# Pooled attention and a two-layer feed-forward on one core: attention in cycles of 4 and 5 key chunks, a new table of issue times, preparation in four banks, weights converted in the last pair, second phase in passes of 2, 4, 4, 4, 2

## The chip, the cores and the metric

One core of one Trainium2 chip runs the whole program. The metric is device time in microseconds (us), the median of several executions. The engines are named as the profile names them: PE (matrix engine, PEld its weight loads), DVE (vector), ACT (scalar), POOL (GpSimd), SP (which issues DMAs).

## The reference

```python
# q, k, v: (4, 8, 1152, 64) float32; w_in (512, 2048), w_out (2048, 512)
q_pool = q.reshape(B, H, S // 2, 2, D).mean(axis=3)        # 576 query rows a head
scores = 1/np.sqrt(D) * np.matmul(q_pool, k.transpose(0, 1, 3, 2))
scores = scores - np.max(scores, axis=-1, keepdims=True)
attn = np.exp(scores)
attn = attn / (np.sum(attn, axis=-1, keepdims=True) + 1e-09)
attn_out = np.matmul(attn, v)                               # (4, 8, 576, 64)
x = attn_out.transpose(0, 2, 1, 3).reshape(2304, 512)
h = np.maximum(x @ w_in, 0.0)
out = (h * h) @ w_out                                       # (2304, 512)
```

## The kernel before, in words

**First phase.** Two heads make a pair, and there are 16 pairs, two heads side by side on the partitions. A pair is worked in two halves `e` of 288 query rows, each over 9 key chunks of 128 keys.
- Preparation: `load_q`, `load_k`, `load_v` issue the DMAs on SP, `pool_q` (L217, L219) adds neighbouring query rows on POOL. `prep` transposes keys and queries on PE into one PSUM bank `t`, `prep_high` (ACT, L256) writes the rounded high part and `prep_low` (DVE, L261, L263) the rest. Five such units a pair share the one bank with the row-maximum transposes and the row sums.
- Row maxima: `maxes` (PE, L285) multiplies queries by keys into one PSUM buffer `m` of two banks, `max_left` (DVE, L297, L293) reduces it; 12 such units a pair. `max_fin` (DVE, L301) ends them, `max_turn` (PE, L308) transposes the result and `max_rows` (ACT, L315) writes it as the rows `mm`.
- Scores: `scores` (PE, L326) makes a chunk's scores minus the maximum in one of two buffers `s`, eight matmuls; `expo` (ACT, L331) writes exp into `p`.
- `pv` (PE, L337) multiplies `p` by v and `pv_x` (ACT, L350) takes the result to `xt`. `add` (POOL, L361) sums the `p` of a half over its chunks, `total` (PE, L366), `total_x` (ACT, L371) and `recip` (DVE, L375) make the reciprocal row sums, `scale_x` (POOL, L380) applies them.
- While a pair's scores run, the next pair is prepared and its maxima are taken.

**The order** of all this is written out by hand: `at(key, ...)` gives each step a time in units of a cycle (here 3 chunks, 6 cycles a pair), with fractions from the table `AT`; a step named in `after` moves a key up. The steps are issued sorted by key, and every engine works its own steps in that order.

**Weights.** The weights arrive as 64-bit numbers; a unit is 128 columns of `w_in` or 128 rows of `w_out`, 32 units in all. `load_raw` loads one, `convert` makes float32 of it in six DVE operations (L119 to L133) and one POOL addition (L135), `split_w` divides it into a high part (ACT, L145) and a low part (DVE, L146).  Eight units are converted in the first phase, from cycle 14 on, one operation a cycle.

**Second phase.** Tokens stand in 5 tiles, one of 256 and four of 512; `f` runs over 16 blocks of 128 hidden columns. `split_x` (ACT L152, DVE L153) divides a token tile into high and low parts. `layer1(i, f)` is 12 matmuls (L507), then a square of the positive part (ACT L509, DVE L511), split again (ACT L514, DVE L515); `layer2` (L543) follows two steps later and adds into four PSUM banks over the blocks of a pass. A pass is 4 blocks (`FP`) over all 5 token tiles, then the sums are copied (ACT L549) or added (DVE L551) to `part`. The units of the next pass are converted during a pass.

Of the kernel before, what the change touches and what calls it, by code (L numbers as in the profile page):

```python
# [21 lines left out]
    s=(.04, .16, .28), e=(.16, .31, .46),  # L22
    xa=0., ra=.06, xb=.40, rb=.47, rf=.50,
    ma=.46, ha=.62, la=.75, mb=.90, hb=1.0, lb=1.34,
    pv=(.55, .66, .77), px=.95,
    a0=.65, a1=.65, a2=.70, a3=.75,
    sm=.92, sc=1.02, sr=(1.8, 2.8), sx=2.9,
    c0=14, cp=1.0, cf=.80,
)
WARM = 16  # L30
# [4 lines left out]
def kernel(  # L35
# [22 lines left out]
    G = 3  # L58
    W = G * P
# [9 lines left out]
    def run(ctx, exact):  # L69
# [6 lines left out]
        xt = [xpool.tile([P, KD, TW[i]], F32, name=f"xt{i}") for i in range(NB)]  # L76

        def x_cols(c0, n):
            while n:
                i, o = divmod(c0 - TW[0] + TB, TB)  # L80
                o -= 0 if i else TB - TW[0]
                m = min(n, TW[i] - o)
                yield i, o, m
                c0 += m
                n -= m
# [7 lines left out]
        FP = 4  # L93
        FX = 2
# [64 lines left out]
        with ExitStack() as a:  # L159

            kq = a.enter_context(tc.tile_pool(name="kq", bufs=1))
            ptp = a.enter_context(tc.tile_pool(name="ptp", bufs=5))
# [15 lines left out]
            PM = [kq.tile([P, 2, NT5, G], F32, name=f"pm{i}") for i in range(2)]  # L178
# [56 lines left out]

            def prep(n, u):
                t = bank(n)
                if u < G:
                    kt = ld_["k", n]
                    for i in range(G):  # L240
                        nc.tensor.transpose(out=t[:, i * P:(i + 1) * P], in_=kt[:, u * G + i].rearrange("p h d -> p (h d)"), identity=ident)
                    b_[n, u] = t[:, :W], [x[:, u * W:(u + 1) * W] for x in KK[n % 2]], 1.0
                else:
                    qp, qpl = qp_[n]
                    rs = range(NR - 1) if u == G else range(NR - 1, NR)
                    for i, r in enumerate(rs):
                        nc.tensor.transpose(out=t[:, i * P:(i + 1) * P], in_=qp[:, r].rearrange("p h d -> p (h d)"), identity=ident)  # L247
                    w = len(rs) * P
                    if u > G:
                        nc.tensor.transpose(out=t[:, w:w + NL], in_=qpl.rearrange("p h d -> p (h d)"), identity=ident[0:NL, 0:NL])  # L250
                        w += NL
                    b_[n, u] = t[:, :w], [x[:, rs[0] * P:rs[0] * P + w] for x in QQ[n % 2]], QS

            def prep_high(n, u):
                x, (hi, lo), sc = b_[n, u]
                nc.scalar.activation(out=hi, in_=x, func=ACTF.Copy, scale=sc)  # L256

            def prep_low(n, u):
                x, (hi, lo), sc = b_.pop((n, u))
                if u < G:  # L260
                    nc.vector.tensor_tensor(out=lo, in0=x, in1=hi, op=ALU.subtract)  # L261
                else:
                    nc.vector.scalar_tensor_tensor(out=lo, in0=x, scalar=sc, in1=hi, op0=ALU.mult, op1=ALU.subtract)  # L263


            units = [(t, g) for t in range(3) for g in range(2)] + [((0, 1, 2), 2)] + \
                    [(t, g) for t in range(3, NT5) for g in range(2)] + [((3, 4), 2)]
# [4 lines left out]
            def maxes(n, u):  # L272
                ts, g = units[u]
                if n == 0 and u < 8 and u % 3:
# [31 lines left out]
            def max_turn(n, e):  # L306
                t = bank(n or e)
                nc.tensor.transpose(out=t[:, :P], in_=NM[n % 2].rearrange("p h t -> p (h t)"), identity=ident)  # L308
# [18 lines left out]

            def expo(n, e, c):
                if c % G == 0:
                    p_[n, e, c // G] = ptp.tile([P, G, 2, NH], F32, tag="p", name="p")  # L330
                nc.scalar.activation(out=p_[n, e, c // G][:, c % G], in_=s_.pop((n, e, c))[:, :, :NH], func=ACTF.Exp)  # L331

            def pv(n, e, c):
                if c == 0:
                    pv_[n, e] = vps.tile([P, 512], F32, tag="pv", name="pv")
                for h in range(2):
                    nc.tensor.matmul(out=pv_[n, e][rows(h), :NH], lhsT=ld_["v", n][:, h, c, :],  # L337
                                     rhs=p_[n, e, c // G][:, c % G, h, :], start=(c == 0), stop=(c == NC - 1))
# [280 lines left out]
```

## Time and profile before

| | |
|---|---|
| median of 3 runs | 1027.32 us (1018.22 to 1029.48) |
| profiled execution, its own time | 1035.19 us |
| its span, first to last instruction | 1033.1 us |
| PE busy / weight loads busy | 913.3 us / 661.8 us |
| DVE, ACT, POOL busy | 669.8, 445.5, 437.4 us |
| mean granted clock of PE | 0.934 |

The busy times are sums over two phases with different limits, so they are read by stretch: the rows of the section below come from the table of stretches, the timeline, and the groups of instructions. A matmul's row ends where its last column is modelled to leave; what the engine needs for one is read from the start of one row to the start of the next. In brackets stands how long an engine sat idle before a row, and what ended that.

### The profile page before, as it was taken

The numbers are of one execution on the slowest core, as the hardware profiler recorded it, in microseconds if no ns is written. First come the engines' busy times: TensorE is split into PE (matmuls) and PEld (weight loads), VectorE is DVE, ScalarE is ACT, GpSimd is POOL, SyncE is SP. The second block draws the span as 40 slices with busy tenths as digits, with TensorE's granted clock in tenths as the row PEclk, the third lists the DMA queues.
The fourth block names the chain that finished last, engine by engine and source line by source line (L and its number), as shares of the span: only waits on it lengthen the run. The fifth ranks groups of instructions, "written<-read, shape, count | busy, mean of one in ns | idle before, by whom it ended". The sixth has DMA issues, their size and how long they took to land.

```text
span 1033.1 us, 15093 instructions
## 1 busy us (share of the span) xinstructions
PE 913.3 (88%) x6162; PEld 661.8 (64%) x6162; DVE 669.8 (65%) x839; ACT 445.5 (43%) x872; POOL 437.4 (42%) x246
## 2 busy tenths in 40 slices
PE   6828888889888888888988987999999999999996
PEld 4515555555455555555655656888888888888885
DVE  5135687877878878756555648764877597754433
ACT  2515545545545444445554554444433333233321
POOL 0623676776766857767676781110111010100000
PEclk6958999989899899899998997999999999999999
DMA  4122113302302311211221000111111011000112
GB/s 114 24 69 67 47 44 90 81 27 74 90 23 67 89 47 24 70 46 26 68 70 44 2 1 21 62 61 42 41 62 41 22 55 48 22 1 21 42 41 85
DMA packets 61967, 50.87 MB, mean 49 GB/s; under 512 B 39104, under 2 KB 49344, under 8 KB 61888
## 3 DMA queue, kind: packets, MB, share of 16 engines
q1 hardware_dynamic: 61088, 48.50, 16.5%
q10 hardware_dynamic: 800, 1.31, 0.4%
q8 instruction: 50, 0.82, 0.3%
q14 instruction: 29, 0.24, 0.1%
HBM read 45.09 MB, written 4.72 MB: 48 GB/s over the span
## 4 chain that ended last, share of the span: by engine, by line
PE 68%; POOL 10%; ACT 9%; DVE 9%; issue 2%; DMA 1%; SPq 0%; ACTq 0%; POOLq 0%
PE o L543 18%; PE h L507 18%; PE pv L337 13%; PE s L326 9%; POOL ts L361 8%; ACT p L331 6%; PE m L285 4%; DVE pm L297 3%; DVE r L133 3%; POOL qp L217 2%; ACT j L228 2%; PE t L366 2%; PE t L247 1%; DVE a L119 1%; ACT kk L256 1%
## 5 line engine op out<-in xcount | busy, mean ns | idle before, releaser
L297 DVE TENSOR_REDUCE pm<-m 128x2 f32<-128x1024 f32 x155 | 189.3, 1221 | 119.1 <-PE m L285 118.5
L331 ACT ACTIVATE p<-s 128x576 f32<-128x576 f32 x288 | 177.3, 650 | 102.6 <-PE s L326 102.6
L326 PE MATMUL s<-qq,kk 64*128 64x288 f32 x1728 | 174.0, 309 | 25.7 <-ACT p L331 25.7
L337 PE MATMUL pv<-p,vt 128*64 128x288 f32 x1152 | 185.5, 464 | 0.0
L361 POOL TENSOR_TENSOR ts<-p 128x1728 f32<-128x1728 f32 x32 | 123.9, 3873 | 139.5 <-ACT p L331 139.5
L543 PE MATMUL o<-wo,gh 128*128 128x512 f32 x576 | 177.8, 390 | 1.2 <-ACT gh L514 1.2
L507 PE MATMUL h<-xhi,wi 128*128 128x512 f32 (+1 forms) x600 | 172.0, 370 | 5.0 <-ACT wi L145 5.0
L326 PEld LDWEIGHTS s<-qq,kk 64*128 64x128 f32 x1728 | 137.8, 189 | 54.2 <-ACT p L331 47.6
L135 POOL TENSOR_TENSOR r<-r,h 128x512 f32<-128x512 f32 x32 | 42.3, 1321 | 251.1 <-DVE r L133 183.1
L361 POOL TENSOR_TENSOR ts<-ts,p 128x1728 f32<-128x1728 f32 x32 | 123.8, 3869 | 27.9 <-ACT p L331 27.9
L507 PEld LDWEIGHTS h<-xhi,wi 128*128 128x128 f32 x600 | 110.8, 190 | 25.5 <-ACT wi L145 5.9
L285 PE MATMUL m<-kk,qq 64*128 64x512 f32 (+1 forms) x470 | 93.9, 425 | 34.6 <-DVE pm L297 26.3
L337 PEld LDWEIGHTS pv<-p,vt 128*64 128x64 f32 x1152 | 82.2, 150 | 65.5 <-issue 30.2
L543 PEld LDWEIGHTS o<-wo,gh 128*128 128x128 f32 x576 | 107.1, 188 | 23.3 <-ACT gh L514 1.9
L543 PE MATMUL o<-wo,gl 128*128 128x512 f32 x288 | 112.1, 389 | 0.0
L507 PE MATMUL h<-xlo,wi 128*128 128x512 f32 (+1 forms) x300 | 110.7, 369 | 0.0
L361 POOL TENSOR_TENSOR ts<-ts 128x576 f32<-128x576 f32 x64 | 94.1, 1470 | 4.0
L514 ACT CAST gh<-g 128x512 fp32r<-128x512 f32 (+1 forms) x80 | 46.3, 579 | 110.1 <-PE o L543 65.9
L285 PEld LDWEIGHTS m<-kk,qq 64*128 64x128 f32 x470 | 44.4, 198 | 71.5 <-DVE pm L297 36.1
L515 DVE TENSOR_TENSOR gl<-g,gh 128x512 fp32r<-128x512 f32 (+1 forms) x80 | 54.3, 678 | 52.1 <-ACT gh L514 51.7
L326 PE MATMUL s<-mm,oner 64*128 64x288 f32 x576 | 87.3, 294 | 0.0
L375 DVE RECIPROCAL r<-r 128x144 f32<-128x144 f32 x64 | 64.5, 1030 | 21.2 <-ACT r L371 21.2
(93 smaller groups left out, 1028.9 us busy)
## 6 DMA issues: line engine op xcount, KB each, us to landing
kt<-in_k_dram SPq DMA_DIRECT2D x32, 288.0 KB, 4.3
vt<-in_v_dram SPq DMA_DIRECT2D x16, 576.0 KB, 3.9
qt<-in_q_dram SPq DMA_DIRECT2D x16, 512.0 KB, 3.9
raw<-in_moe_w_in_dram SPq DMA_DIRECT2D x16, 512.0 KB, 3.8
raw<-in_moe_w_out_dram SPq DMA_DIRECT2D x16, 512.0 KB, 3.5
out_dram<-part SPq DMA_DIRECT2D x8, 256.0 KB, 2.6
out_dram<-part ACTq DMA_DIRECT2D x10, 128.0 KB, 3.3
out_dram<-part SPq DMA_DIRECT2D x10, 128.0 KB, 2.7
```

Of the source, the lines that this page charges most:

```text
L135: nc.gpsimd.tensor_tensor(out=r, in0=r, in1=h.bitcast(F32), op=ALU.add)
L285: nc.tensor.matmul(out=m[:, h, o], lhsT=l[rows(h), TQ[t]:TQ[t] + P], rhs=r[rows(h), ks], start=(x == 0), stop=(x == len(terms) - 1))
L297: nc.vector.tensor_reduce(out=pm[:, :, ts, g], in_=m, op=ALU.max, axis=AX.X, negate=True)
L326: nc.tensor.matmul(out=s[:, h, :NH], lhsT=l[rows(h)], rhs=r[rows(h)], start=(i == 0), stop=(i == 3))
L331: nc.scalar.activation(out=p_[n, e, c // G][:, c % G], in_=s_.pop((n, e, c))[:, :, :NH], func=ACTF.Exp)
L337: nc.tensor.matmul(out=pv_[n, e][rows(h), :NH], lhsT=ld_["v", n][:, h, c, :], rhs=p_[n, e, c // G][:, c % G, h, :], start=(c == 0), stop=( ...
L361: nc.gpsimd.tensor_tensor(out=o, in0=x, in1=y, op=ALU.add)
L375: nc.vector.reciprocal(out=x, in_=x)
L507: nc.tensor.matmul(out=h, lhsT=w, rhs=x, start=(m == 0), stop=(m == len(mm) - 1))
L514: nc.scalar.copy(out=gh, in_=g)
L515: nc.vector.tensor_tensor(out=gl, in0=g, in1=gh, op=ALU.subtract)
L543: nc.tensor.matmul(out=acc[i][t], lhsT=g, rhs=w, start=(first and m == 0), stop=(last and m == 2))
```

## The change: what it does

- A half's 9 chunks are worked in two cycles, of 4 and 5 chunks (`CYCLE`), so a pair has 4 cycles instead of 6. `p` has 3 buffers of 5 chunks instead of 5 buffers of 3.
- Every kind of step has its own time in `AT`, and `pool_q`, the loads and the preparation of the next pair get other places.
- Keys and queries are prepared in 4 uses of the bank `t` (4, 4, 1 + 3 and 2 transposes) instead of 5, and the fourth also holds the maxima of the pair before, so `t` is used 7 times a pair instead of 9. The key buffer is double.
- A half's `p` is summed by a four-chunk, a one-chunk, a two-chunk and a one-chunk addition instead of 3, 3, 1 and 1; in the last pair by eight one-chunk additions.
- `xt` is tiled by batch, so that a half's result is one piece; `split_x` splits by batch instead.
- Four units are converted in the first phase, all in the last pair; the passes of the second phase have 2, 4, 4, 4 and 2 blocks. `split_x` of the next token tile stands at a pass's second block, as before.

```diff
-    s=(.04, .16, .28), e=(.16, .31, .46),
+    e=-0.666, h0=-1.798, h1=-0.099, h2=0.09, h3=-0.731, l0=-2.259, l1=-1.892, l2=-1.181, l3=-2.391, m0=3.23,
...
+CYCLE = 4, 5
-        xt = [xpool.tile([P, KD, TW[i]], F32, name=f"xt{i}") for i in range(NB)]
+        xt = [xpool.tile([P, KD, NQ], F32, name=f"xt{i}") for i in range(B)]
-        FP = 4
-        FX = 2
+        PASS = [2, 4, 4, 4, 2]
+        P0 = [sum(PASS[:i]) for i in range(len(PASS) + 1)]
+        WB = 6
-            ptp = a.enter_context(tc.tile_pool(name="ptp", bufs=5))
+            ptp = a.enter_context(tc.tile_pool(name="ptp", bufs=3))
-                t = ld.tile([P, NC, 2, D], F32, tag="k", name="kt")
+                t = ld.tile([P, NC, 2, D], F32, tag="k", name="kt", bufs=2)
+            def adds(n):
+                if n == NP - 1:
+                    return [(c, slice(0, 1), (0, 0) if c == 1 else None, at_[c]) for c in range(1, NC)]
+                return [(7, slice(0, 4), (0, 0), (1, 0)), (8, slice(0, 1), None, (1, 4)),
+                        (8, slice(0, 2), None, 2), (8, slice(0, 1), None, 1)]
-            NCY = 6
+            R = len(CYCLE)
+            NCY = 2 * R
+            CU = 2 * PASS[0]
-                    at(pre - 5.5, ("lq", n), load_q, n, after=[("pq", n - 1)])
+                    at(pre + .6, ("lq", n + 1), load_q, n + 1, after=[("pq", n)])
-                at(pre - .3 if n else -20, ("pq", n), pool_q, n, after=[("lq", n), ("prep", n - 1, 3), ("prep", n - 1, 4), ("sq", n - 1, 2)])
+                    at(base + A["pq"], ("pq", n + 1), pool_q, n + 1,
+                       after=[("lq", n + 1), ("prep", n, 2), ("prep", n, 3), ("sq", n, 1), ("sq", n, 2)])
-            for u in range(2 * FP):
-                at(A["c0"] + u * NCV * A["cp"] - 2, ("lr", u), load_raw, u, after=[("cv", u - 2, NCV - 1)])
+            for u in range(CU):
+                at(last - 3 + u, ("lr", u), load_raw, u, after=[("cv", u - 2, NCV - 1)])
                 for j in range(NCV):
-                    at(A["c0"] + (u * NCV + j) * A["cp"] + A["cf"], ("cv", u, j), convert, u, j, after=[("lr", u), ("cv", u, j - 1)])
+                    at(last + (u * NCV + j) * 4.2 / (CU * NCV), ("cv", u, j), convert, u, j, after=[("lr", u), ("cv", u, j - 1)])
-        steps = [(i, p0 + f) for p0 in range(0, KF, FP) for i in range(NB) for f in range(FP)]
+        steps = [(i, f, p) for p in range(len(PASS)) for i in range(NB) for f in range(P0[p], P0[p + 1])]
+            every = (NB * PASS[p - 1] - 2) / m
-                if f % FP == 1 and n + FP < len(steps):
+                if f == P0[p] + 1 and n + PASS[p] - 1 < len(steps):
                     split_x((i + 1) % NB, xh_p)
```

Three places in the order of issue. First PE, from the last scores of pair 0 to the transpose of pair 1's first maxima (`nm`); kk and qq of 105, 106, 109, 110 are pair 0's, 107 and 111 pair 1's. Before:

```order
L326 MATMUL s<-mm_118,oner 128x288 x2
L337 MATMUL pv<-p,vt 64x288 x6
L241 MATMUL t<-ident,kt 128x128 x9
L247 MATMUL t<-ident,qp 128x128 x4
L250 MATMUL t<-ident,qpl 128x64
L285 MATMUL m<-kk_107,qq_111 128x512 x12
L285 MATMUL m<-kk_107,qq_111 128x128 x6
L285 MATMUL m<-kk_107,qq_111 128x512 x2
L308 MATMUL t<-ident,nm_116 128x128
```

The same engine in the changed kernel, in the first half of pair 0's scores (kk_104, qq_108 pair 0's, kk_106, qq_110 pair 1's):

```order
L331 MATMUL s<-mm_116,oner 128x288 x2
L290 MATMUL m<-kk_104,qq_108 128x512 x2
L242 MATMUL t<-ident,kt 128x128
L248 MATMUL t<-ident,qp 128x128 x3
L290 MATMUL m<-kk_106,qq_110 128x512 x2
L331 MATMUL s<-qq_108,kk_104 128x288 x2
```

Pair 1's transposes and maxima moved from behind all scores of pair 0 to between them.

Second POOL, one pair of the steady part. Before (`qp` is the addition of neighbouring query rows, `ts` the sum over chunks, `xt` the scaling):

```order
L361 TENSOR_TENSOR ts<-p 128x1728
L361 TENSOR_TENSOR ts<-ts,p 128x1728
L361 TENSOR_TENSOR ts<-ts 128x576
L217 TENSOR_TENSOR qp<-qt 128x2x4x64
L219 TENSOR_TENSOR qpl<-ql 64x128
L361 TENSOR_TENSOR ts<-ts 128x576
L380 TENSOR_TENSOR xt_77<-xt_77,r 128x288
```

And in the changed kernel:

```order
L214 TENSOR_TENSOR qp<-qt 128x2x4x64
L216 TENSOR_TENSOR qpl<-ql 64x128
L374 TENSOR_TENSOR ts<-p 128x2304
L374 TENSOR_TENSOR ts<-ts,p 128x576
L374 TENSOR_TENSOR ts<-ts 128x1152
L374 TENSOR_TENSOR ts<-ts 128x576
L392 TENSOR_TENSOR xt_76<-xt_76,r 128x288
```

`qp` moved from behind three additions of a half to ahead of all four.

Third DVE in the last pair, from the first maxima's end (`nm`) on. Before:

```order
L301 TENSOR_REDUCE nm_116<-pm_114 128x2x2
L153 TENSOR_TENSOR xlo<-xt_76,xhi 128x1024
L375 RECIPROCAL r<-r 128x144
L146 TENSOR_TENSOR raw<-r,raw 128x512
L375 RECIPROCAL r<-r 128x144 x5
```

In the changed kernel (L110 to L124 are the six operations of `convert`, L302 the reductions, the last row the end of the second half's maxima):

```order
L110 TENSOR_SCALAR a<-raw 128x512
L302 TENSOR_REDUCE pm_113<-m 128x2
L112 TENSOR_SCALAR a<-a 128x512
L115 TENSOR_SCALAR a<-a 128x512
L302 TENSOR_REDUCE pm_113<-m 128x2
L118 SCALAR_TENSOR_TENSOR h<-raw,a 128x512
L388 RECIPROCAL r<-r 128x144
L122 TENSOR_SCALAR a<-h 128x512
L124 SCALAR_TENSOR_TENSOR r<-raw,a 128x512
L388 RECIPROCAL r<-r 128x144
L110 TENSOR_SCALAR a<-raw 128x512
L306 TENSOR_REDUCE nm_115<-pm_113 128x2x2
```

A whole unit and the start of the next now stand ahead of the second half's maxima, and three more units stand between these and the split of the first weight block.

## Rows read from the trace of the kernel before

**Rows 1.** Timeline of DVE: ends of pairs' first maxima (start, us, engine, operation).
```profile
20.82 0.16 DVE L301 TENSOR_REDUCE nm<-pm 128x6 f32<-128x18 f32 x1
83.13 0.16 DVE L301 TENSOR_REDUCE nm<-pm 128x6 f32<-128x18 f32 x1
111.84 0.17 DVE L301 TENSOR_REDUCE nm<-pm 128x6 f32<-128x18 f32 x1
...
410.50 0.17 DVE L301 TENSOR_REDUCE nm<-pm 128x6 f32<-128x18 f32 x1
...
585.37 0.17 DVE L301 TENSOR_REDUCE nm<-pm 128x6 f32<-128x18 f32 x1
```

**Rows 2.** Table of stretches: length, busy (x instructions) by engine, PEclk, DMA share, GB/s.
```profile
480.00:515.00 35.00, 30.75 (x280) 20.07 (x280) 20.50 (x24) 18.24 (x40) 24.81 (x14) 0.95 0.19 52
...
634.00:732.00 98.00, 98.00 (x457) 82.04 (x456) 65.38 (x109) 42.40 (x71) 11.18 (x8) 1.00 0.15 49
...
830.00:929.00 99.00, 98.32 (x456) 82.03 (x455) 74.17 (x117) 35.18 (x53) 10.50 (x8) 1.00 0.10 33
929.00:1025.00 96.00, 96.00 (x435) 79.64 (x433) 42.13 (x60) 26.83 (x40) 0.00 (x0) 1.00 0.12 39
```

**Rows 3.** Timeline between pairs 0 and 1 (POOL and PE).
```profile
55.99 1.26 POOL L217 TENSOR_TENSOR qp<-qt 128x512 f32<-128x512 f32 x1
...
59.52 0.90 PE L241 MATMUL t<-ident,kt 128*128 128x128 f32 x3 [9.02 <-DVE kk L261]
```

**Rows 4.** Timeline of PE behind `pool_q` in a later pair.
```profile
489.46 0.74 PE L247 MATMUL t<-ident,qp 128*128 128x128 f32 x3 [2.47 <-POOL qp L217]
...
490.13 3.12 PE L337 MATMUL pv<-p,vt 128*64 128x288 f32 x12
```

**Rows 5.** Timeline of PE, a cycle in which it hardly waits.
```profile
498.81 0.55 PE L241 MATMUL t<-ident,kt 128*128 128x128 f32 x3
499.29 0.50 PE L285 MATMUL m<-kk,qq 64*128 64x512 f32 x2
499.62 0.56 PE L326 MATMUL s<-qq,kk 64*128 64x288 f32 x6
...
500.15 0.56 PE L326 MATMUL s<-qq,kk 64*128 64x288 f32 x6
...
501.06 0.67 PE L326 MATMUL s<-qq,kk 64*128 64x288 f32 x6 [0.22 <-ACT p L331]
...
502.27 1.68 PE L337 MATMUL pv<-p,vt 128*64 128x288 f32 x12
503.88 0.33 PE L247 MATMUL t<-ident,qp 128*128 128x128 f32 x1
```

**Rows 6.** Groups of DVE, 120 to 420 us: shapes, xcount | busy us, mean ns | idle before.
```profile
L297 DVE TENSOR_REDUCE pm<-m 128x2 f32<-128x1024 f32 x80 | 97.8, 1223 | 46.9 <-PE m L285 46.4
L375 DVE RECIPROCAL r<-r 128x144 f32<-128x144 f32 x33 | 33.4, 1031 | 0.0
L133 DVE SCALAR_TENSOR_TENSOR r<-raw,a 128x512 f32<-128x512 uint32 x7 | 24.6, 3512 | 0.0
```

**Rows 7.** Timeline, a conversion step on DVE beside an addition on POOL.
```profile
163.01 3.88 POOL L361 TENSOR_TENSOR ts<-p 128x1728 f32<-128x1728 f32 x1 [2.59 <-ACT p L331]
...
163.93 3.51 DVE L133 SCALAR_TENSOR_TENSOR r<-raw,a 128x512 f32<-128x512 uint32 x1
```

**Rows 8.** Groups of POOL over the whole span.
```profile
L361 POOL TENSOR_TENSOR ts<-p 128x1728 f32<-128x1728 f32 x32 | 123.9, 3873 | 139.5 <-ACT p L331 139.5
...
L361 POOL TENSOR_TENSOR ts<-ts 128x576 f32<-128x576 f32 x64 | 94.1, 1470 | 4.0
```

**Rows 9.** Groups of DVE in the second phase, from 640 us on.
```profile
L515 DVE TENSOR_TENSOR gl<-g,gh 128x512 fp32r<-128x512 f32 x64 | 45.3, 708 | 48.1 <-ACT gh L514 47.8
...
L153 DVE TENSOR_TENSOR xlo<-xt,xhi 128x2048 fp32r<-128x2048 f32 x15 | 34.4, 2290 | 20.4 <-ACT xhi L152 20.4
...
L133 DVE SCALAR_TENSOR_TENSOR r<-raw,a 128x512 f32<-128x512 uint32 x23 | 15.8, 688 | 0.5
```

More of the change, by code (lines that the diff above doesn't have):

```diff
@@ L151, in split_x @@
             lo = pool.tile([P, KD, TW[i]], F32R, tag="xlo", name="xlo")
-            nc.scalar.copy(out=hi, in_=xt[i])
-            nc.vector.tensor_tensor(out=lo, in0=xt[i], in1=hi, op=ALU.subtract)
+            t, o = sum(TW[:i]), 0
+            while o < TW[i]:
+                e, c = divmod(t + o, NQ)
+                m = min(NQ - c, TW[i] - o)
+                x, h, l = (y[:, :, z:z + m] for y, z in ((xt[e], c), (hi, o), (lo, o)))
+                nc.scalar.copy(out=h, in_=x)
+                nc.vector.tensor_tensor(out=l, in0=x, in1=h, op=ALU.subtract)
+                o += m
             xs[i] = (hi, lo)
@@ L177, in run @@
             TQ = [r * P for r in range(NR)] + [NQ - P]
-            PM = [kq.tile([P, 2, NT5, G], F32, name=f"pm{i}") for i in range(2)]
+            PM = [kq.tile([P, 2, NT5, 3], F32, name=f"pm{i}") for i in range(2)]
             NM = [kq.tile([P, 2, 64], F32, name=f"nm{i}") for i in range(2)]
@@ L237, in prep @@
                 t = bank(n)
[L238 to L252, printed above, removed]
+                hi, lo = 0, 1
@@ new lines, in prep @@
+                kt, (qp, qpl) = ld_["k", n], qp_[n] if u > 1 else (None, None)
+                cs = range(4 * u, 4 * u + 4) if u < 2 else range(8, NC) if u == 2 else ()
+                rs = range(NR - 1) if u == 2 else range(NR - 1, NR) if u == 3 else ()
+                parts, o = [], 0
+                for i in cs:
+                    nc.tensor.transpose(out=t[:, o:o + P], in_=kt[:, i].rearrange("p h d -> p (h d)"), identity=ident)
+                    o += P
+                if o:
+                    parts.append((t[:, :o], [x[:, cs[0] * P:cs[0] * P + o] for x in KK[n % 2]], 1.0))
@@ L266, in run @@
-            units = [(t, g) for t in range(3) for g in range(2)] + [((0, 1, 2), 2)] + \
-                    [(t, g) for t in range(3, NT5) for g in range(2)] + [((3, 4), 2)]
+                for x, (hi, lo), sc in b_.pop((n, u)):
+                    if sc == 1.0:
+                        nc.vector.tensor_tensor(out=lo, in0=x, in1=hi, op=ALU.subtract)
+                    else:
+                        nc.vector.scalar_tensor_tensor(out=lo, in0=x, scalar=sc, in1=hi, op0=ALU.mult, op1=ALU.subtract)
@@ L269, in rows @@
+            units = [(t, g) for g in range(2) for t in range(3)] + [((0, 1, 2), 2)] + \
+                    [(t, g) for g in range(2) for t in range(3, NT5)] + [((3, 4), 2)]
             def rows(h):
@@ new lines, in run @@
+                    at(t + A[f"r{u}"], ("ml", n, u), max_left, n, u, after=[("mx", n, u), ("mr", n - 2, 1)])
+                t = pre + A["m0"] if n else -20
+                at(t - .02, ("mf", n, 0), max_fin, n, 0, after=[("ml", n, u) for u in range(7)])
+                at(t, ("mt", n, 0), max_turn, n, 0, after=[("mf", n, 0)])
+                at(t + A["mr0"], ("mr", n, 0), max_rows, n, 0, after=[("mt", n, 0)])
+                if n < NP - 1:
+                    at(base + A["pq"], ("pq", n + 1), pool_q, n + 1,
+                       after=[("lq", n + 1), ("prep", n, 2), ("prep", n, 3), ("sq", n, 1), ("sq", n, 2)])
+                    unit(n + 1, 3)
@@ L455, in run @@
+            at(last + 2.5, "x0", split_x, 0, xh_0, after=[("sx", H // 2 - 1, 1)])
+            at(last + 4.5, "w0", split_w, 0, cv, "raw", 2, after=[("cv", CU - 1, NCV - 1)])
             nc.vector.tensor_tensor(out=MASK, in0=ident[:, 0:NT5], in1=ident[:, 64:64 + NT5], op=ALU.add)
@@ L535, in layer2 @@
             woh, wol = wo[f][:, 0], wo[f][:, 1]
-            first, last = f % FP == 0, f % FP == FP - 1
+            p = max(x for x in range(len(PASS)) if P0[x] <= f)
+            first, last = f == P0[p], f == P0[p + 1] - 1
             if first:
```

205 lines of the change are left out of this document (103 added, 102 removed).

## Prediction

> **What bounds the kernel now.** The table of stretches comes first, because it shows two phases with different limits. From 634 to 1025 us PE is busy in 98.00 of 98 us, 98.32 of 99 and 96.00 of 96, at full granted clock [rows 2]: the second phase is 391 us of matmuls that stand close behind each other, and nothing but fewer matmuls shortens it. Before that, no engine is full. Between 480 and 515 us PE has 30.75 us of 35, POOL 24.81, DVE 20.50, ACT 18.24, at a clock of 0.95 [rows 2]. So here the order decides, and the next view is the timeline of one event that every pair has once, the end of its first maxima on DVE [rows 1]. Pair 1 comes 62.3 us behind pair 0, pair 2 only 28.7 us behind pair 1. Then eight pairs take (410.50 - 111.84) / 8 = 37.3 us each and the last five (585.37 - 410.50) / 5 = 35.0 us. Three questions follow: why 62, why 37 and 35, and why once 28.7.
>
> The 62 are a start in series: POOL reaches pair 1's `qp` at 55.99, behind pair 0's additions, and PE stands for 9.02 us until 59.52 before it can prepare pair 1 [rows 3]. The 35 hold a smaller copy of this: in each pair PE waits 2.47 us for `qp`, and the pv behind it take 3.12 us for twelve [rows 4] where they take 1.61 elsewhere, from 502.27 to 503.88 [rows 5]; PE had stood still, PE had stood still, and the stretch's mean clock of 0.95 [rows 2] says that part of it ran at the low level of 1.2 GHz.. Together 4 us. In the eight pairs at 37.3 one unit of weights is converted in each pair, and its steps are long beside POOL: L133 takes 3.51 us in the first phase [rows 6] and 0.69 in the second [rows 9]. One look shows why: it begins at 163.93, POOL's addition runs from 163.01 to 166.89, and it ends at 167.44, 0.55 us after it [rows 7]. It waits until POOL's instruction in progress is over, and the reductions for the maxima queue behind it. The pair of 28.7 us had neither a wait for `qp` nor conversions.
>
> **The change part by part.** Sums run along the first-maxima ends.
>
> *Start.* Pair 0 goes as before to its first maxima, with one more 1024-wide reduction (1.22 us [rows 6]) ahead: 20.8 + 1.2 = 22. Pair 1 then no longer waits for pair 0's additions (the first order excerpt). Its bound is the loop of one `m` buffer: a unit's matmuls last 0.50 us [rows 5], its reduction 1.22, with the hand-over 1.8 us a unit, ten units and two short ones at 1.5, 21 us, and five `prep_low` on the same queue, half a reduction each at most (up to 512 columns against 1024): 24 us. It ends at 46 instead of 83.
>
> *A steady pair.* What PE needs, start to start [rows 5]: 18 score chunks of 0.53, 12 maxima units of 0.33, pv 6 times 1.61, 16 transposes of 0.16, row sums 1.1 (eight matmuls at pv's rate): 26.9 us. That is the lower bound. The upper bound is 35.0, if nothing of the new order helps. `qp` now stands ahead of a half's additions, a cycle before PE wants it, so the 4 us go. A wait for exp at every third chunk remains possible (0.22 us and a restart [rows 5]), but maxima units now stand between the chunks. Against that, units follow each other at places after two score chunks, 1.4 us where the `m` loop wants 1.8: 0.4 us four times, and a reciprocal (1.03 us [rows 6]) ahead of a reduction. Some 2 us on 26.9 is 28.9, and the nearest row is the pair without `qp` wait and conversions, 28.7. I take 28.7, fourteen times, 402 us.
>
> *What costs nothing.* The regrouped additions have the same elements: 2.1 ns an element from 3.87 us for 1728 and 1.47 for 576 [rows 8], so 5.1 + 1.5 + 2.7 + 1.5 = 10.7 us a half, as 3.87 + 3.87 + 1.47 + 1.47 was. POOL has some 25 us a pair, under 28.7. Three `p` buffers are enough as long as the four-chunk addition ends before the next half's second group of exp begins; it has about five chunks' time, 7 us, for 5.1. One bank use less, the loads' places and the second key buffer lie beside PE. In the last pass the extra `split_x` and additions lie under PE, which leaves DVE more than half idle there (42.13 of 96 [rows 2]).
>
> *The last pair.* Here the conversions come, 24 DVE steps, and the pass of 4 blocks shows what they cost alone: DVE 74.17 us with eight units and 42.13 without [rows 2], 4.0 us a unit with its 0.7 us split, so 3.3. DVE has four reductions 4.9, four reciprocals 4.1, 4 x 3.3 = 13.2, a half-width xlo 1.2 and a split 0.7: 24 us without waits. The first unit stands beside pair 14's additions, 10.7 us of POOL, and each step waits for the instruction in progress: 10 us. The other 18 steps meet additions of 1.47 us, half of one on average: 13 us. Sum 47 us from the first maxima to the first weight block. The second half's maxima stand behind more than a unit (the third excerpt), so PE, with 30 us of its own work in this stretch, will stand still there for several us. Bounds: 38 (PE's 30, then row sums and splits) and 60 (every step waits for a whole addition, 26 us instead of 13). The Trainium skill (GPSIMD Engine Reference, Key points) says that POOL shares its SBUF interfaces with DVE, and that they contend where a DVE instruction works in a two-port mode or has two SBUF inputs. L133 has two, and the trace agrees with 3.51 against 0.69 us. By that rule the xlo and the split, with two SBUF inputs each, would wait too, half an addition each: 1.5 us more and a forecast of 909; no row here shows these two beside POOL, and the sum leaves it out.
>
> *First pass.* A block costs PE 24.6 us (391 plus 3 for narrow matmuls ahead of 634, by 16), so two cost 49. DVE has eight units and splits 32 us [rows 2], g and gl of two blocks at 0.71 each for eight wide steps and half of it for two narrow ones [rows 9], 12.8, five xlo of 2.29 with one at half [rows 9], 10.3, and the end of the attention (four reciprocals, three splits, small steps) 7: 62 us. DVE is the longer, so this pass costs 62. Bounds 49, if the pipeline of two steps takes it up, and 72, if each step also waits for POOL. The remaining 14 blocks are 345 us, as in the trace, with 3 us to fill; the tail behind the last matmul, 1033.1 - 1025 = 8.
>
> *Sum.* 46 + 402 + 47 + 62 + 345 + 3 + 8 = 913 us of span, 915 with the 2.1 us that this execution has around its span, against its own 1035.2. The runs' median is 1027.3, 0.992 of that: 908 us.
>
> **Rivals.**
>
> *The gaps stay.* The fillers meet DVE's queue, which carries reductions, `prep_low` and reciprocals in a new interleaving, and a pair stays at 35.0. For it: DVE has 20.5 us plus waits in every pair. Against it: one pair ran in 28.7 with the old order. Price 14 x 6.3 = 88 us: 995.
>
> *PE has more room.* POOL would be the next bound, some 24.6 us a pair: 14 x 4.1 = 57 us less, 850. Against it: start to start, PE's own rows sum to 26.9. The Trainium skill (Trainium Kernel Development and Optimization, Performance Expectations) holds that busy time of matmuls is a poor measure and that of weight loads a good one. By that rule PE is not near its limit in the attention (20.07 of 35 us of weight loads [rows 2]) and the pair would fall to POOL's sum, hence this rival's time; the trace agrees in so far as the second phase, where PE never stands, has 82 of 98.
>
> *Slower than before.* The bank `t` has one buffer, and each of its seven uses waits for ACT's copy and DVE's subtraction, which now stand behind four- and five-chunk runs of exp and behind reductions. PE's queue stops with it. It decides from 38 us a pair: (1035 - 915) / 14 = 8.6 over 28.7 is 37.3, and 1 per cent is 0.7 more. That needs 5.4 us a use; in the dense cycle two uses (keys, then `nm`) lie between 498.81 and 503.88, where the third begins [rows 5], 2.5 us each. Time 1040 or more.
>
> *The conversions weigh more at the end.* Both upper bounds, 60 and 72: 23 us more, 931. It lies within the forecast's own range.
>
> **How the numbers follow.** The forecast, with the conversions' bounds and a pair of 27.3 to 31, has 0.72; its own range is 880 to 940. The gaps that stay, wholly or by half (a pair over 31): 0.17. More room for PE: 0.08. Slower: 0.03. To hold 8 in 10 the range takes in a pair of up to 31.7 us, 950; below it stays at 880. Faster by over 1 per cent covers all but the last and a share of the worst gaps: 0.95; within 1 per cent 0.02, slower by over 1 per cent 0.03. One per cent is about what a measurement of this kernel can tell from no change.
>
> **What would show it.** The ends of the first maxima: pair 1's near 46 us, then steps of 28.7. PE's wait for `qp` gone from the list of waits. In the last pair L110, L115, L118 and L124 that end just behind a POOL row, and a PE wait of several us at the second `nm`. From the first weight block on, DVE nearly full for about 60 us with gaps on PE, then PE full for 345. The prediction is wrong if steps between maxima stay at 35, if PE is full in the first pass, or if the last pair is not longer than the steady one.

## The result and the profile after

The changed kernel takes 922.83 us (median of 4 runs, 922.6 to 924.33), the kernel before 1028.4 us beside it (4 runs, 1018.22 to 1034.29): a ratio of 0.9006, interval 0.894 to 0.9073. The forecast was 908 us, between 880 and 950. The profiled execution has a span of 921.2 us and took 923.03.

The first view is again the timeline of DVE, at the ends of the first maxima (columns as in [rows 1]; the last row is the second half of the last pair):

```profile
21.98 0.16 DVE L306 TENSOR_REDUCE nm<-pm 128x6 f32<-128x18 f32 x1
47.36 0.17 DVE L306 TENSOR_REDUCE nm<-pm 128x6 f32<-128x18 f32 x1
76.15 0.17 DVE L306 TENSOR_REDUCE nm<-pm 128x6 f32<-128x18 f32 x1
...
450.27 0.17 DVE L306 TENSOR_REDUCE nm<-pm 128x6 f32<-128x18 f32 x1
469.43 0.15 DVE L306 TENSOR_REDUCE nm<-pm 128x4 f32<-128x12 f32 x1
```

Pair 1 comes at 47 instead of 83 us, and all steps after it are alike: (450.27 - 47.36) / 14 = 28.78 us, where 37.3 and 35.0 stood [rows 1]. The table of stretches (columns as in [rows 2]) shows what carries this:

```profile
120.00:160.00 40.00, 39.60 (x375) 26.70 (x376) 27.82 (x31) 25.73 (x56) 32.99 (x16) 1.00 0.27 73
...
500.00:510.00 10.00, 6.75 (x27) 5.39 (x26) 8.66 (x17) 6.84 (x11) 2.25 (x3) 0.50 0.08 27
510.00:562.00 52.00, 51.01 (x239) 42.30 (x239) 45.96 (x72) 27.34 (x48) 9.01 (x6) 0.99 0.21 67
...
680.00:914.00 234.00, 233.51 (x1060) 194.07 (x1058) 151.53 (x239) 77.96 (x120) 14.19 (x11) 1.00 0.12 37
```

In the steady pairs PE is busy for 39.60 of 40 us at full granted clock, where it had 30.75 of 35 [rows 2]. Two of PE's waits are behind this, over the whole span (us in total, times, longest), in the kernel before:

```profile
PE s L326 <- ACT p L331: 25.7, 94, 1.0
PE t L247 <- POOL qp L217: 19.2, 13, 2.5
```

In the changed kernel the wait for exp is all but gone, and that for `qp` stands there once, at the start (1.0 us):

```profile
PE s L331 <- ACT p L341: 1.3, 4, 0.6
```

The last pair pays for it. Three engines in it, PE, then POOL and DVE (start, us, engine, line, operation, in brackets the idle time before it and what ended it):

```profile
469.64 0.47 PE L313 MATMUL t<-ident,nm 128*128 128x128 f32 x1 [5.66 <-DVE nm L306]
...
499.04 1.23 PE L379 MATMUL t<-ts,one 128*64 128x288 f32 x4 [8.47 <-POOL ts L374]
500.20 0.80 PE L537 MATMUL h<-xhi,raw 128*128 128x256 f32 x2
```
```profile
453.08 5.10 POOL L374 TENSOR_TENSOR ts<-p 128x2304 f32<-128x2304 f32 x1 [1.98 <-ACT p L341]
...
471.55 8.36 POOL L374 TENSOR_TENSOR ts<-ts,p 128x576 f32<-128x576 f32 x5
```
```profile
454.73 3.74 DVE L110 TENSOR_SCALAR a<-raw 128x512 int32<-128x512 int32 x1
...
471.90 1.79 DVE L118 SCALAR_TENSOR_TENSOR h<-raw,a 128x512 int32<-128x512 int32 x1
473.73 1.52 DVE L122 TENSOR_SCALAR a<-h 128x512 int32<-128x512 int32 x1
475.28 1.79 DVE L124 SCALAR_TENSOR_TENSOR r<-raw,a 128x512 f32<-128x512 uint32 x1
...
481.53 2.45 DVE L149 TENSOR_TENSOR xlo<-xt,xhi 128x1024 fp32r<-128x1024 f32 x1
...
497.66 1.88 DVE L137 TENSOR_TENSOR raw<-r,raw 128x512 fp32r<-128x512 f32 x1
```

From its first maxima to the first weight block (500.20) the last pair takes 49.9 us. L110 ends at 458.47, 0.29 us behind POOL's long addition; from 471.55 on five additions and five conversion steps go in lockstep, each step about one addition (8.36 / 5 = 1.67 us) long. PE waits 5.66 us for the second maxima, which stand behind conversion steps, and 8.47 us for POOL's last row sum.

Where the time went, span against span (1033.1 and 921.2): the start to pair 1 gives 35.8 us, the 14 pairs 502.2 - 402.9 = 99.3. The last pair takes back 49.93 - 30.46 = 19.5, and the second phase 3.7 (from the first weight block to the end, 421.0 against 417.3).

### The profile page after: what moved, and what is told of

Its sections match the earlier page's. It is cut to its first block, busy times and chain, and to the rows that moved or that the text cites. A ratio compares the mean times of both kernels' runs of the same rounds, so it can differ in the third digit from the quotient of the medians.

```text
span 921.2 us, 15238 instructions
## 1 busy us (share of the span) xinstructions
PE 873.8 (95%) x6162; PEld 650.8 (71%) x6162; DVE 652.5 (71%) x877; ACT 448.3 (49%) x876; POOL 442.8 (48%) x238
## 4 chain that ended last, share of the span: by engine, by line
PE 79%; DVE 13%; ACT 3%; issue 2%; POOL 2%; DMA 1%; SPq 0%; ACTq 0%; POOLq 0%; DVEq 0%
PE h L537 18%; PE o L574 18%; PE s L331 16%; PE pv L348 15%; PE m L290 7%; DVE pm L302 3%; PE t L242 2%; PE t L379 2%; POOL r L126 1%; DVE r L124 1%; DVE a L110 1%; DVE a L115 1%; ACT p L341 1%; DVE h L118 1%; PE t L248 1%
## 5 line engine op out<-in xcount | busy, mean ns | idle before, releaser
L302 DVE TENSOR_REDUCE pm<-m 128x2 f32<-128x1024 f32 x154 | 188.5, 1224 | 59.1 <-PE m L290 59.1
L126 POOL TENSOR_TENSOR r<-r,h 128x512 f32<-128x512 f32 x32 | 46.5, 1453 | 302.2 <-DVE r L124 288.3
L374 POOL TENSOR_TENSOR ts<-p 128x2304 f32<-128x2304 f32 (+1 forms) x32 | 157.0, 4905 | 60.4 <-ACT p L341 60.4
L348 PE MATMUL pv<-p,vt 128*64 128x288 f32 x1152 | 156.1, 411 | 0.0
L331 PEld LDWEIGHTS s<-qq,kk 64*128 64x128 f32 x1728 | 130.9, 188 | 34.1 <-issue 19.3
L537 PEld LDWEIGHTS h<-xhi,wi 128*128 128x128 f32 x600 | 112.4, 193 | 27.5 <-ACT wi L136 6.9
L374 POOL TENSOR_TENSOR ts<-ts 128x1152 f32<-128x1152 f32 (+1 forms) x60 | 121.5, 2024 | 4.7
L348 PEld LDWEIGHTS pv<-p,vt 128*64 128x64 f32 x1152 | 77.1, 136 | 58.9 <-issue 14.1
L290 PE MATMUL m<-kk,qq 64*128 64x512 f32 (+1 forms) x468 | 86.0, 398 | 4.6 <-DVE pm L302 2.7
L545 DVE TENSOR_TENSOR gl<-g,gh 128x512 fp32r<-128x512 f32 (+1 forms) x80 | 53.0, 663 | 35.1 <-ACT gh L544 34.7
L539 ACT ACTIVATE r<-h 128x512 f32<-128x512 f32 (+1 forms) x80 | 44.2, 552 | 61.5 <-PE h L537 59.2
L149 DVE TENSOR_TENSOR xlo<-xt,xhi 128x1024 fp32r<-128x1024 f32 (+7 forms) x40 | 57.7, 1444 | 19.5 <-ACT xhi L148 19.5
L541 DVE SCALAR_TENSOR_TENSOR g<-h,r 128x512 f32<-128x512 f32 (+1 forms) x80 | 50.6, 632 | 25.3 <-ACT r L539 25.3
```

What stands on the lines that cost most here:

```text
L126: nc.gpsimd.tensor_tensor(out=r, in0=r, in1=h.bitcast(F32), op=ALU.add)
L149: nc.vector.tensor_tensor(out=l, in0=x, in1=h, op=ALU.subtract)
L290: nc.tensor.matmul(out=m[:, h, o], lhsT=l[rows(h), TQ[t]:TQ[t] + P], rhs=r[rows(h), ks], start=(x == 0), stop=(x == len(terms) - 1))
L302: nc.vector.tensor_reduce(out=pm[:, :, ts, g], in_=m, op=ALU.max, axis=AX.X, negate=True)
L331: nc.tensor.matmul(out=s[:, h, :NH], lhsT=l[rows(h)], rhs=r[rows(h)], start=(i == 0), stop=(i == 3))
L374: nc.gpsimd.tensor_tensor(out=t[:, o], in0=part(x or 0), in1=part(y), op=ALU.add)
```

## The experiments

A variant with one run has no interval; ranges are those of the runs, ratios and their intervals stand against the kernel before, which had a median of 1030 us beside all of them. A difference between two variants is one of medians from separate measurements and has no interval.

**1. Only `qp` earlier, in the kernel before.**

```diff
-                 at(pre - .3 if n else -20, ("pq", n), pool_q, n, ...)
+                 at(pre - .9 if n else -20, ("pq", n), pool_q, n, ...)
```

> The kernel before with one number changed: pool_q's key goes from pre - .3 to pre - .9, so that POOL forms qp ahead of the additions of a half instead of between them; everything else stays. Theory (the prediction's term: the wait of 2.47 us for qp and the slow pv behind it are some 4 us of each pair): the steps between first-maxima ends fall from 37.3 to about 33.5 in the pairs with conversions and from 35.0 to about 31 in the others, the wait for qp leaves the list of waits, and the run takes about 1027 - 13 x 4 = 975 us. Rival (the wait moves): PE waits for the next thing in the same place, the preparation's own chain or DVE's queue, the steps stay within 1 us of 37.3 and 35.0, and the run stays at 1015 to 1030 us.

Measured: 1006.94 us (one run). The first-maxima ends of its later pairs:

```profile
362.54 0.17 DVE L301 TENSOR_REDUCE nm<-pm 128x6 f32<-128x18 f32 x1
400.08 0.17 DVE L301 TENSOR_REDUCE nm<-pm 128x6 f32<-128x18 f32 x1
...
466.10 0.17 DVE L301 TENSOR_REDUCE nm<-pm 128x6 f32<-128x18 f32 x1
496.53 0.17 DVE L301 TENSOR_REDUCE nm<-pm 128x6 f32<-128x18 f32 x1
```

The run lies between the 975 us of the theory and the 1015 of the rival: both hold, each in its own pairs. PE's wait for `qp` falls from 19.2 us in 13 pairs to 1.3 in one. Where no unit is converted, the step falls from 34.7 us (the last four of before) to 30.4, 4.3 us against the 4 of the prediction. Where one is, four of nine steps stay at 36.6 to 37.6 (as 400.08 - 362.54), and the others reach 34.9 to 35.7: there the pair is held whether `qp` is early or not, and the conversion steps are what these pairs have and the others lack. So the two delays covered each other: taking one away leaves the other. In this order of undoing, the 99 us of the 14 pairs are 26 for `qp`, some 52 for the conversions (nine pairs, 325.2 us instead of 9 x 30.4) and some 22 for the rest, 30.4 to 28.8 a pair; the rest (cycles, regrouped additions, key buffer) was not taken apart; what its traces show is that PE's wait for exp, 27.5 us in this run, is 1.3 in the changed kernel.

**2. Score chunks without their fourth product, in the changed kernel.**

```diff
-             for i, (l, r) in enumerate(((kh, qh), (kl, qh), (kh, ql), (ONER, MM[n % 2][e]))):
+             for i, (l, r) in enumerate(((kh, qh), (kl, qh), (kh, ql))):
```

> The changed kernel without the fourth product of a score chunk (mm by oner): it leaves out the subtraction of the row maximum from the scores, so PE has 36 of its 144 score matmuls less in a pair and nothing else differs. In the dense cycle of before a score chunk of eight took 0.53 us, so 18 chunks lose 18 x 0.13 = 2.4 us. Theory (a steady pair of the changed kernel is bounded by PE, busy 39.6 of 40 us): the step between first-maxima ends falls from 28.8 to about 26.4 and the run from 923 to about 890. Rival 1 (the loop of m buffer and DVE paces the pair, and PE's busy time holds waits in the matmuls): the step stays at 28.5 to 28.8 and the run at 915 to 923. Rival 2 (POOL is next close behind, 33 of 40 us busy with its own waits): the step stops at about 27.5, the run at 905.

Measured: 909.12 us (one run). Two of its first-maxima ends, twelve pairs apart, and the largest PE wait from 120 to 400 us (us in total, times, longest), here and then in the changed kernel:

```profile
74.14 0.17 DVE L306 TENSOR_REDUCE nm<-pm 128x6 f32<-128x18 f32 x1
...
409.76 0.17 DVE L306 TENSOR_REDUCE nm<-pm 128x6 f32<-128x18 f32 x1
```
```profile
PE m L290 <- DVE pm L302: 5.2, 16, 0.4
```
```profile
PE m L290 <- DVE pm L302: 1.3, 8, 0.2
```

The step is 335.62 / 12 = 27.97 us: of the 2.4 us taken from PE only 0.8 came out. PE's visible waits for `m` and the key transposes grew from 1.3 to 9.2 us in those 280 us, 0.8 more a pair. So PE did bound the steady pair, but the loop over the one `m` buffer lies less than a microsecond behind it; the theory's 26.4 and the first rival's 28.5 are both wrong. The second rival's 27.5 comes nearest in time, but not by its cause: no wait of PE for POOL stands among those of these 280 us. The remaining 0.8 us of the 2.4 stay within PE's busy rows, and what they are is open.

**3. Conversions spread over six steady pairs.**

```diff
-                     at(last + (u * NCV + j) * 4.2 / (CU * NCV), ("cv", u, j), convert, ...)
+                     at(14.8 + u * NCV + j, ("cv", u, j), convert, ...)
```

> The changed kernel with the 24 conversion steps taken out of the last pair and put one to a cycle into six steady pairs (the fourth to the ninth), four steps in each. Theory (a conversion step costs what it waits for POOL's five-element additions, and DVE has no slack at the places where the maxima's reductions queue): the last pair falls from 49 to 36 to 38 us, the six pairs grow by 1.5 to 4 us each from 28.8, and the run stays within 912 to 935 us. Rival (conversions in the last pair were the error, the steady pairs have room for them, with DVE at 28 of 40 us): the six pairs stay at 28.8 to 29.3, the last falls to 37, and the run takes 909 to 912 us.

Measured: 936.2 us (one run). A step in one of the six pairs (POOL, DVE), the ends around it, and PE at the end of the last pair:

```profile
151.39 5.09 POOL L374 TENSOR_TENSOR ts<-p 128x2304 f32<-128x2304 f32 x1 [2.30 <-ACT p L341]
```
```profile
132.99 0.17 DVE L306 TENSOR_REDUCE nm<-pm 128x6 f32<-128x18 f32 x1
...
153.10 3.94 DVE L118 SCALAR_TENSOR_TENSOR h<-raw,a 128x512 int32<-128x512 int32 x1
156.96 0.68 DVE L298 TENSOR_REDUCE pm<-m 128x4 f32<-128x512 f32 x1
...
165.45 0.17 DVE L306 TENSOR_REDUCE nm<-pm 128x6 f32<-128x18 f32 x1
```
```profile
513.15 1.23 PE L379 MATMUL t<-ts,one 128*64 128x288 f32 x4 [7.06 <-POOL ts L374]
```

The six pairs take 31.6 to 33.6 us, 2.8 to 4.9 more each and 24 us together; a reduction of `m` queues behind the step that waits for POOL, and PE behind it. The last pair falls to 40.9 us, not to 37: with no conversion in it, POOL's own chain of additions holds PE for 7.06 us. So 24 steps cost 24 us in steady pairs and 9 in the last one. The theory is right in kind, but the steady pairs and the last one both come out longer than it has them, and the run 1 us above its range; the rival, free room in the steady pairs, falls.

**4. Row sums of the last pair on PE.**

```diff
-                 if n == NP - 1: return [(c, slice(0, 1), ...) for c in range(1, NC)]
+                 if n == NP - 1: return []
...
+                     for c in range(NC):
+                         for h in range(2):
+                             nc.tensor.matmul(out=t[rows(h), :NH], lhsT=ONE, rhs=p_[n, e, r][:, i, h, :], ...)
...
+                     if (n, e) == (NP - 1, 0):
+                         t = base + 2.95
```

The last two lines move the first half's row sums behind its last exp.

> The changed kernel with the row sums of the last pair formed by PE (nine pairs of ones-by-p matmuls a half in one bank instead of one pair over POOL's sum), so that POOL has no additions of p in that pair; the conversions stay where they are. It costs PE some 16 x 2 matmuls, at pv's 0.134 us each 4.3 us. Theory (the last pair is long because each conversion step waits until POOL's addition in progress is over, 13 us on average by the prediction): from the 19th step on and partly before, the steps take 0.7 instead of 1.4 to 2 us, first maxima of the last pair to first weight block falls from 49.3 to 40 to 43 us, and the run to 914 to 918 us. Rival (DVE's sum of work there is long by itself and the steps stretch for other reasons): it stays at 47 us or more and the run at 921 to 928 us.

Measured: 920.26 us (919.67 to 920.61), 0.8937 of before (0.8907 to 0.8967). PE, then DVE's last split:

```profile
478.97 4.54 PE L382 MATMUL t<-p,one 128*64 128x288 f32 x36
...
491.73 4.54 PE L382 MATMUL t<-p,one 128*64 128x288 f32 x36
496.19 0.51 PE L545 MATMUL h<-xhi,raw 128*128 128x256 f32 x2
```
```profile
488.66 1.28 DVE L137 TENSOR_TENSOR raw<-r,raw 128x512 fp32r<-128x512 f32 x1
```

DVE is done at 489.9, 40.5 us behind the first maxima (449.44) instead of 49.3: without POOL's additions the steps shrink as the theory has it. The first weight block follows only at 46.7 us, because PE now has 9 us of row sums and still its wait for the second maxima (4.36 us). The mechanism is right; the size is not, because a second engine was close.

**5. Passes of 2, 3, 4, 4, 3.**

```diff
-        PASS = [2, 4, 4, 4, 2]
+        PASS = [2, 3, 4, 4, 3]
```

> The changed kernel with the second phase in passes of 2, 3, 4, 4, 3 blocks instead of 2, 4, 4, 4, 2, so that the first pass, which has 2 blocks, prepares six units of weights instead of eight and the last pass gets six. Theory (the prediction's term for the first pass: it is bound by DVE, 62 us, of which a unit's conversion and split are 4 us): the first pass loses 2 x 4 = 8 us of DVE's work, down to PE's 49 plus a start, so 5 to 8 us go, and the later passes hide the units as before; the run takes 915 to 918 us. Rival 1 (the first pass is already paced by PE and the start of the second phase by ACT's splits and DMAs, so units there cost nothing): 921 to 924 us. Rival 2 (the pass of 3 blocks prepares 8 units in three quarters of the time and becomes the bound instead): 923 to 930 us.

Measured: 919.35 us (918.74 to 920.37), 0.8931 (0.8867 to 0.8994). The stretch in which the first pass ends, in the changed kernel and here (columns as before):

```profile
562.00:570.00 8.00, 4.78 (x23) 3.75 (x23) 7.83 (x17) 3.55 (x9) 1.44 (x1) 0.92 0.28 95
```
```profile
562.00:570.00 8.00, 7.69 (x35) 5.97 (x33) 6.12 (x12) 4.43 (x8) 2.78 (x1) 1.00 0.22 66
```

Two units less for DVE, 8 us of work, give 3.5 us between the medians: one PE wait of 3.22 us for a weight split goes. That is between theory and first rival, and not a pass bound by DVE throughout. Of the 3.1 us between the two profiled executions 1.0 stands ahead of the last pair's first maxima (449.25 against 450.27), where the kernels are alike, and 2.0 behind the first weight block. The second rival shows too, in small: behind the first pass PE now waits for DVE's sums into `part` (from 500 to 600 us; in the changed kernel 1.1 us, once):

```profile
PE o L574 <- DVE part L582: 3.1, 2, 2.5
```

**6 and 7. Conversions behind the second maxima, alone and with the row sums on PE.**

```diff
-                     at(last + (u * NCV + j) * 4.2 / (CU * NCV), ("cv", u, j), convert, ...)
+                     at(last + 1.25 + (u * NCV + j) * 2.95 / (CU * NCV), ("cv", u, j), convert, ...)
```

> The changed kernel with the conversions of the last pair begun 1.25 cycles into it, behind the second half's maxima, instead of at its start; the order of everything else stays. In the changed kernel PE waited 5.66 us for the second maxima behind them. Theory (DVE's sum of work and waits sets the end of the last pair, not PE's wait): the PE wait of 5.66 us goes, the conversions start later and end when they did, and only what the first unit waited beside the long additions (3.74 and 2.74 us for L110 and L115) is won; the run takes 918 to 921 us. Rival 1 (PE's wait is in the path): about 5.5 us less, 916 to 918 us. Rival 2 (DVE's end is in the path and starts later): 923 to 928 us.

> The changed kernel with both: conversions begun 1.25 cycles into the last pair and that pair's row sums formed by PE from all nine chunks. With the sums on PE alone DVE ended its last conversion 39 us behind the first maxima, while PE, with 2 x 4.5 us of row sums and a wait of 4.4 us for the second maxima, reached the first weight block 47 us behind them. Theory (PE has become the bound of that stretch): the wait of 4.4 us goes and the run takes 915 to 917 us against 920.3 with the sums on PE alone. Rival (DVE becomes the bound again, since its 24 steps start 10 us later): 919 to 925 us.

Measured: 925.13 us (921.81 to 925.64; 0.8989, 0.8926 to 0.9052) alone, and 911.99 (911.26 to 912.43; 0.8859, 0.8796 to 0.8921) together. PE in the first of them:

```profile
498.75 1.23 PE L379 MATMUL t<-ts,one 128*64 128x288 f32 x4 [16.87 <-POOL ts L374]
```

DVE and PE in the second:

```profile
471.32 1.22 DVE L149 TENSOR_TENSOR xlo<-xt,xhi 128x1024 fp32r<-128x1024 f32 x1 [1.65 <-ACT xhi L148]
...
484.55 0.68 DVE L137 TENSOR_TENSOR raw<-r,raw 128x512 fp32r<-128x512 f32 x1
```
```profile
489.77 0.50 PE L545 MATMUL h<-xhi,raw 128*128 128x256 f32 x2
```

Alone, the wait of 5.66 us goes, but PE then stands 16.87 us for POOL's row sum: POOL and DVE, each waiting for the other's instruction in progress, set the end, and nothing is won. The 24 steps take 31.3 us instead of 34.4 but begin 7.8 us later behind the first maxima (12.2 against 4.5), so the second rival holds, with 923 to 928 us; the profiled execution is the fastest of the four. Together, PE reaches the first weight block 40.7 us behind the first maxima, 9.3 us sooner than in the changed kernel, and DVE is done 4.5 us before it. The 24 steps take 15.8 us in all, against 34.4 in the changed kernel and 13.2 by the rows of the second phase. That is 3 us more gain than the theory's 915. Some 2 us of it lie in this stretch, 40.7 us against 46.7 in experiment 4 where the theory took off 4.4: PE waits for nothing in it but exp, 1.0 us in all from 455 us on. The rest lies behind the first weight block and was not taken apart.

**8. POOL adds the first four chunks, PE the rest.**

```diff
-                     return []
+                     return [(c, slice(0, 1), (0, 0) if c == 1 else None, at_[c]) for c in range(1, CYCLE[0])]
```

> As the kernel with late conversions and row sums on PE, but POOL adds the first four chunks of each half of the last pair and PE sums that result and the other five chunks: six pairs of ones matmuls a half instead of nine, 3.0 instead of 4.5 us, and three POOL additions a half instead of eight. Theory (with sums on PE that engine bounds the last pair, and short additions early in a half stand in nobody's way): 2 x 1.5 = 3 us less than with all sums on PE, 912 to 914 us. Rival (the conversion steps wait behind the six additions, 1.45 us each, and DVE's end moves behind PE's): 917 to 921 us.

Measured: 914.99 us (913.71 to 915.65), 0.8887 (0.8824 to 0.8951), slower than all nine chunks on PE. PE and DVE:

```profile
491.24 0.39 PE L546 MATMUL h<-xhi,raw 128*128 128x256 f32 x1 [2.89 <-DVE raw L137]
```
```profile
490.50 0.68 DVE L137 TENSOR_TENSOR raw<-r,raw 128x512 fp32r<-128x512 f32 x1
```

Six short additions are enough to bring DVE's last split behind PE again: the rival's mechanism, at less than its price.

**9 and 10. Late conversions, sums on PE, and other passes.**

```diff
-        PASS = [2, 4, 4, 4, 2]
+        PASS = [2, 3, 4, 4, 3]      (9)
+        PASS = [2, 3, 3, 4, 4]      (10)
```

> Late conversions and row sums on PE in the last pair, together with passes of 2, 3, 4, 4, 3 blocks. Apart they measured 912.0 and 919.4 us against 922.8 for the changed kernel. Theory (the two act in different stretches, the last pair and the first pass): the gains add, 922.8 - 10.8 - 3.4 = 908.6 us, between 907 and 910. Rival (the gain of the passes came from DVE being late at the start of the second phase, which the earlier end of the conversions already gives back): 911 to 913 us.

> The same with passes of 2, 3, 3, 4, 4 blocks: the second pass, of 3 blocks, prepares six units instead of eight, and the last pass has four blocks with nothing to prepare behind it. With 2, 3, 4, 4, 3 PE still waited 3.1 us in the second pass for DVE's additions into part. Theory (DVE's load in the second pass causes those waits): 2 units less there, 905 to 907.5 us. Rival (the waits come from the additions into part at a pass's end, whatever it prepares): the same as with 2, 3, 4, 4, 3 within 1 us.

Measured: 910.04 us (909.25 to 911.2; 0.8838, 0.8811 to 0.8865) and 908.82 (907.78 to 909.88; 0.8826, 0.8799 to 0.8853). The gains add for the most part: 2 of the 3.5 us remain with passes of 2, 3, 4, 4, 3. The last one, the fastest kernel here, is 14 us under the changed kernel. Its 1.2 us over the ninth fit neither expectation well, and PE's wait for the sums into `part` is not less (4.2 us in all against 3.9), so DVE's load in the second pass is not shown as the cause.

## Why the prediction was right, and where it was off

| Stretch | Forecast, us | Measured, us |
|---|---|---|
| Start to the end of pair 1's first maxima | 46 | 47.4 |
| 14 pairs | 402 | 402.9 |
| Last pair, to the first weight block | 47 | 49.9 |
| First pass, to PE's restart at 567.74 | 62 | 67.5 |
| The other 14 blocks, with 3 to fill | 348 | 345.8 |
| Tail behind the last matmul | 8 | 7.7 |
| Span | 913 | 921.2 |

*The start and the pairs* came as forecast, for the reasons given in the main: `qp`'s wait is gone, and experiment 1 prices it at 4.3 us where the sum had 4. Of the start's 1.4 us over, 1.1 belong to this execution: its granted clock is 0.66 in the first 30 us, and experiment 7, whose edit acts in the last pair alone, has 1.00 there and ends pair 1's first maxima at 46.28. The 28.7 was taken as 26.9 of PE's work and some 2 us of the `m` loop. Measured are 28.78 with PE at 39.60 of 40, so PE is busy for 28.5 us of a pair, and its waits for `m` that the profile shows are 0.13 us a pair (1.3 in 280). Experiment 2 shows both limits close together, but how the 1.6 us over 26.9 divide between PE's own work and the `m` loop is open. The rival in which gaps stay has no row for it.

*More room for PE*, the rival that the Trainium skill (Trainium Kernel Development and Optimization, Performance Expectations) stood for, fell. The Trainium skill calls busy time of matmuls a bad measure there of how close a kernel is to its limit, and that of weight loads a good one. The latter reads 26.70 of 40 us in a pair that got only 0.8 us shorter when 2.4 us of matmuls left. For the time that this order of work can still give, matmuls at 39.60 of 40 were the nearer measure, and the trace disagrees with what the prediction drew from that rule.

*The last pair*: the steps of the first unit took 10.2 us, 6.9 over their 3.3 (forecast 10 over), the other 18 steps 24.2, 14.3 over their 9.9 (forecast 13). The xlo and the split with two SBUF inputs waited too, 2.45 us against 1.22 and 1.88 against 0.68 without POOL beside them (experiment 7), 2.4 us together. This is what the sum left out because no row showed it. So 23.6 us of waits against 23; the rest of the 2.9 us is 1.9 in which DVE stood idle for `m` at the start, and 0.7 between its last split and the weight block. The mechanism holds: the steps shrink as soon as POOL's additions go (experiments 4 and 7). The Trainium skill (SBUF — State Buffer, SBUF: two separate sides) describes it as a lock: between a POOL instruction and a DVE instruction in a two-port mode or with two SBUF inputs, whichever starts first has the shared ports for its whole instruction, and the other stands. The trace agrees, with L118, which has two such inputs, at 3.94 us, ended 0.56 us behind POOL's addition (experiment 3); DVE's reductions from PSUM, 1.23 us beside POOL as without it, do not wait. What the sum didn't see is that POOL's own chain keeps the last pair at 40.9 us even with nothing to convert (experiment 3); its lower bound of 38 was PE's alone. In the changed kernel itself the two ends lie together: POOL's last sum lets PE go on at 499.04, DVE's split ends at 499.54, and the weight block stands behind PE's own row sums at 500.20.

*The first pass* is the step that failed, though its time came out: its last matmul ends at 561.27, 61.1 us behind the first weight block, against 62. "DVE is the longer, so this pass costs 62" is wrong in its cause, and the near hit is luck. DVE had about the work that the sum gave it, 60.02 us from the first weight block to 567.74, but it did not hold PE: from 510 to 562 us PE is busy for 51.01 of 52 us, with weight loads 42.30 of 52, near the 194.07 of 234 where nothing stops it, and the prediction itself named a full PE as what would refute it. PE's own 49 us grew by other things: 10 us from 500 to 510 with PE at 6.75 and a granted clock of 0.50, which costs some 3.4 us (an estimate, half of the 6.75); a gap of 3.01 us in them for a weight split of ACT's, and two of 0.98 and 0.25 us; and 2.9 us of the second pass's narrow matmuls, two blocks of which stand between the first pass's last ones (1.44 us each, from 551.15 to 552.59). That makes 59.5 of the 61.1. What DVE's load does cost comes behind the pass (PE, with the pass's last matmul first, then ACT, POOL and DVE):

```profile
560.88 0.39 PE L574 MATMUL o<-wo,gl 128*128 128x512 f32 x1
...
567.74 0.39 PE L537 MATMUL h<-xhi,wi 128*128 128x256 f32 x1 [3.22 <-ACT wi L136]
```
```profile
567.07 0.62 ACT L136 CAST wi<-r 128x512 fp32r<-128x512 f32 x1 [2.44 <-POOL r L126]
```
```profile
565.60 1.44 POOL L126 TENSOR_TENSOR r<-r,h 128x512 f32<-128x512 f32 x1 [4.16 <-DVE r L124]
```
```profile
564.76 0.69 DVE L124 SCALAR_TENSOR_TENSOR r<-raw,a 128x512 f32<-128x512 uint32 x1
```

PE stands 3.22 us for the last unit's split, which waits for POOL's addition and this for the last conversion step of DVE, busy for 7.83 of 8 us there. So DVE was the longer by some 3 us, where the sum had 13, and experiment 5, with 8 us less for DVE, won about that. In the table the row to 567.74 also holds this wait and three narrow blocks of the second pass; with the row below it, 413.3 us stand against 410.

*The scale* did as much. The terms came out 8.2 us short in span; the factor 0.992, from the profiled execution of before to its median, took off another 7. The changed kernel's profiled execution, 923.03, lies at its median of 922.83. The factor belonged to the kernel before, whose runs spread over 16 us, and not to this one.

## What to carry to other kernels

Work that waits for another engine's instruction in progress costs most where a short queue stands behind it: 24 conversion steps cost 24 us beside the maxima's reductions and 9 in a pair that another engine stretches anyway; once the other engine's additions are gone, they take 2.6 us more than their own length. Moving one of two coupled delays can gain nothing (experiment 6, and four pairs of experiment 1); try both before dropping either. Before calling a stretch bound by the engine with the larger sum, list the second sum too, for experiments 2, 3, 4 and 8 all ran into it.

## What the runs showed of the hardware

Two things were not expected. The 14 steps between first maxima in the changed kernel differ by 0.03 us at most (28.77 to 28.80), and the runs of each variant that has several stay within 4 us of each other, while the kernel before spreads over 1018 to 1034 us. Its PE stands for `qp` in 13 pairs, and its runs differ in the granted clock: 0.958 in the one of 1019.82 us, 0.934 to 0.946 in those above 1030, against 0.970 to 0.981 in the changed kernel's. That the clock makes the spread was not shown. And the first weight blocks run at a granted clock of 0.50, the level of 1.2 GHz, behind PE's stand of 8.47 us: there four row-sum matmuls take 1.23 us, against 0.66 for the first half's at 487.49. In experiment 7, where PE doesn't stand ahead of them, the first weight matmuls take 0.50 us a pair instead of 0.80.
